# Attention and two gated layers on one core: loads of queries, keys and values moved to POOL's queue, and the order at the last stage's start and end changed

## The chip, the cores and the metric

The kernel runs on one core of a Trainium2 chip. The metric is the device time of one execution in microseconds (us). The median of three runs is 1690.28 us.

## What is computed

All arrays are float32. There are 8 x 576 = 4608 tokens with 8 heads of 64 columns; attention looks only inside chunks of 64 tokens. Its output goes through a layer with a squared relu and then through a layer with a gate.

```
scores = scale * np.matmul(q_c, k_c.transpose(0, 1, 2, 4, 3))      # chunks of 64 x 64
attn = np.exp(scores - max); attn = attn / (sum + 1e-09)
x = attn @ v_c                                   # 4608 x 512
h = np.maximum(x @ w_in, 0.0);  x = h * h @ w_out        # w_in 512 x 2048, w_out 2048 x 512
g = x @ w_gate;  val = x @ w_val                 # 512 x 1536 each
out = (g * (1.0 / (1.0 + np.exp(-g))) * val) @ w_out2    # 1536 x 512
```

## The kernel before

The 4608 tokens are nine blocks of 512. `sets` holds block 0 alone and then four pairs of blocks; a pair is worked on together, since its product with a weight is made by a scheme of seven products for eight (roles 1 to 7 of a `Pair`, and in the last stage roles 1, 5, 6, 2, 7, 4, 3 in `Last`). Every float32 product is three matmuls of 128x512 (lines 464 to 466: high weight by high data, low by high, high by low), so each operand is first split into `hi` (ACT, line 154) and `lo` (DVE, line 157).

The stages follow each other: a start in which the weights w_in are prepared and block 0 and the first pair go through attention; the up product with w_in for each set, and *beside* it the attention of the set after it; the down product with w_out; the products with w_gate and w_val; and the last stage with w_out2 (`Last`). Results between stages go through memory: `g` by ACT's DMA queue, nearly everything else by SP's.

Attention works on units of 256 tokens, four to a pair of blocks. For a unit, `attn_qk` loads q and k (line 324, 512 KB each), `attn_products` makes the scores s by 64 small matmuls (line 340), DVE and ACT make e from it, POOL multiplies e by the reciprocal sums (line 372, e<-e,rec), DVE transposes e to z and ACT copies it to p, with four small DMAs p<-z (line 419), `attn_v` loads v (line 329), and `attn_values` makes the outputs xps by 64 small matmuls (line 439). The table `WHEN` and the function `attention_step` say beside which quarter of which weight each of these steps stands; `EARLY` is 6, the number of units in block 0 and the first pair, which are done in the start. Units from 6 on belong to the second, third and fourth pair: 12 units.

PE's order is that of the code (`ordered(ET.PE)`). On the other engines and on the DMA queues a scheduler sets the order when the program is built; each engine and each queue then runs its row strictly in that order, and an entry that waits holds up all behind it. SP's row holds, beside the loads of q, k and v, the loads W<-wi of prepared weights (line 230, `load_combo`, 1792 KB, asked for by `Products.ask`), which wait until PE has done with the buffer, the stores wi<-W of weights (line 223) and the p<-z copies.

The last stage takes its operands from memory (`Last.load`, line 875, tiles h) and its weights V by `load_last` (lines 285 and 291). `Last.make` builds the operands of the product that comes next; `take`, made by `turned_out`, adds (line 518, o), transposes to z (line 847), and stores the finished half in four DMAs (line 853).

Of the kernel before, what the change touches and what calls it, by code (L numbers as in the profile page):

```python
# [28 lines left out]
def attention_mlp_mlp_kernel(  # L29
# [29 lines left out]
    nc = tc.nc  # L59
# [11 lines left out]
    sets = [(0,)] + [(b, b + 1) for b in range(1, nb, 2)]  # L71
# [12 lines left out]
    def duo(name, dtype=F32):  # L84
        return big.tile([P, 2, BLOCK], dtype, tag="big", name=name)

    def one(name):
        return small.tile([P, BLOCK], F32, tag="t", name=name)
# [191 lines left out]
    def load_last(product, apart=False):  # L280

        r = ROLES[product]
        if not apart:
            v = wp.tile([P, n2, 2, half], F32R, tag="W", name="V")
            nc.sync.dma_start(out=v.bitcast(F32), in_=vdram[r])
            last_weights[product] = [v[:, i] for i in range(n2)]
            return
        last_weights[product] = []
        for i in range(0, n2, 2):
            v = big.tile([P, 2, 2, half], F32R, tag="big", name="V")  # L290
            nc.sync.dma_start(out=v.bitcast(F32), in_=vdram[r][:, i:i + 2])
            last_weights[product] += [v[:, 0], v[:, 1]]

    class Work:
# [5 lines left out]
        def add(self, steps):  # L300
            self.queue.append(steps)
# [15 lines left out]
    EARLY = upb * (1 + len(sets[1]))  # L317
    at, vs = {}, {}
    xraw = {}

    def attn_qk(u):
        tiles = [duo("q"), duo("k")]
        for t, src in zip(tiles, (q, k)):
            nc.sync.dma_start(out=t, in_=src[2 * u:2 * u + 2].rearrange("n p c -> p n c"))
        at[u] = tiles

    def attn_v(u):
        vt = duo("v")
        nc.sync.dma_start(out=vt, in_=v[2 * u:2 * u + 2].rearrange("n p c -> p n c"))
        vs[u] = vt  # L330

    def attn_products(u):
# [128 lines left out]
    def three(ps, left, right, first, last, on=False):  # L461

        (lh, ll), (rh, rl) = left, right
        nc.tensor.matmul(out=ps, lhsT=lh, rhs=rh, start=first, stop=False, skip_group_check=on)  # L464
        nc.tensor.matmul(out=ps, lhsT=ll, rhs=rh, start=False, stop=False, skip_group_check=on)  # L465
        nc.tensor.matmul(out=ps, lhsT=lh, rhs=rl, start=False, stop=last, skip_group_check=on)  # L466

    def block_product(ps, w, i, x, first, last, on=False):
        for c in range(2):
            cols = slice(c * P, (c + 1) * P)  # L470
            three(
                ps,
                (w[:, 0, ROLES[i], cols], w[:, 1, ROLES[i], cols]),
                (x[0][:, c, :], x[1][:, c, :]),
                first and c == 0,
                last and c == 1,
                on,
            )
# [41 lines left out]
    class Pair:  # L520
# [6 lines left out]
        def product(self, ps, i, first):  # L527
            block_product(ps, self.w, i, self.ops[i], first, True, not first)
# [201 lines left out]
    up1 = Products(keys1, moving1, 2, 1, lambda key: squared)  # L730

    def x_sums(n):
        up1.ops[n] = Operands()
        up1.ops[n].sums([xraw.pop(b) for b in sets[n]])
# [103 lines left out]
    def turned_out(bs):  # L838
        z = [[big.tile([P, BLOCK // SQ, 2, SQ], F32, tag="big", name="z") for _ in range(2)] for _ in bs]
        left = [[2, 2] for _ in bs]  # L840

        def take(i, j, e, ps, r):
            if r is not None:
                o = one("o")
                add(o, ps, r)
                ps = o
            nc.vector.transpose(out=z[j][e][:, :, i, :], in_=ps.rearrange("p (b t) -> p b t", t=SQ))
            left[j][e] -= 1
            if left[j][e] == 0:
                rows = out[bs[j] * BLOCK:(bs[j] + 1) * BLOCK, :]  # L850
                rows = rows.rearrange("(b r) (q e c) -> q e r b c", r=SQ, q=4, e=2)
                for qd in range(4):
                    nc.sync.dma_start(
                        out=rows[qd, e],
                        in_=z[j][e][qd * SQ:(qd + 1) * SQ].rearrange("p b i t -> p b (i t)"),
                    )

        return take
# [4 lines left out]
    class Last:  # L863
# [37 lines left out]
                }[p])  # L901
            self.ops[n, p] = ops

        def product(self, ps, n, p, op, first, last=True, on=False):
            w, ops = last_weights[p], self.ops[n, op]
            for i in range(n2):
                hi, lo = ops[i // 2]
                for e in range(2):
                    cols = slice(e * P, (e + 1) * P)
                    three(  # L910
                        ps[e],
                        (w[i][:, 0, cols], w[i][:, 1, cols]),
                        (hi[:, i % 2, :], lo[:, i % 2, :]),
                        first and i == 0,
                        last and i == n2 - 1,
                        on,
                    )
# [14 lines left out]
        def run(self, m):  # L932
            n, p = self.seq[m]
            if p == 1:
                self.take = turned_out(sets[n])
            if len(sets[n]) == 1:
                if p == 1:
                    self.y = self.two("py")
                    self.product(self.y, n, 1, 1, True, False)
                elif p == 5:  # L940
                    self.y1 = self.two("py")
                    self.product(self.y1, n, 5, 1, True, False)
                elif p == 2:
                    self.product(self.y, n, 2, 2, False)
                    self.take_all(0, 0, self.y, None)
                else:
                    self.product(self.y1, n, 4, 4, False)
                    self.take_all(1, 0, self.y1, None)
            elif p == 1:
                self.x = self.two("px")  # L950
                self.product(self.x, n, 1, 1, True)
                self.r1 = self.kept(self.x, "r1")
            elif p == 5:
                self.z = self.two("pz")
                self.product(self.z, n, 5, 5, True)
            elif p == 6:
                self.product(self.x, n, 6, 6, False, on=True)
                self.u2 = self.kept(self.x, "u2")
            elif p == 2:
                y = self.two("py")  # L960
                self.product(y, n, 2, 2, True)
                self.take_all(0, 0, y, self.r1)
            elif p == 7:
                self.product(self.x, n, 7, 7, False, on=True)
                self.take_all(1, 1, self.z, self.kept(self.x, "u3"))
            elif p == 4:
                self.product(self.x, n, 4, 4, False, on=True)
                self.take_all(1, 0, self.x, None)
            else:
                self.product(self.z, n, 3, 3, False, on=True)  # L970
                self.take_all(0, 1, self.z, self.u2)

    down1, down2 = Down(g1dram, n1), Last()

# [24 lines left out]
    def beside1(n, m):  # L999
        def at_quarter(i):  # L1000
            t = 4 * m + i
            attention_step(n + 1, t)
            attention_step(n + 2, t - LAST)
            if t == 2:
                up1.ops[n].make(3)
            if n + 1 < len(sets):
                if t == 24:
                    x_sums(n + 1)
                if t - LAST in OPS:
                    up1.ops[n + 1].make(*OPS[t - LAST])  # L1010
            else:
                if t % 2 == 0:
                    work.step(1)
                if t == LAST - 8:
                    down1.begin()
                if t == LAST - 4:
                    down1.split(0)

        return at_quarter
# [104 lines left out]
    last = down2  # L1124
    load_last(2)
    load_last(4)
    load_last(6)
    with ordered(ET.PE):
        for m, (n, p) in enumerate(last.seq):
            if n + 1 < len(sets):  # L1130
                after = sets[n + 1]
                if p == 1:
                    last.load(after[0], 0)
                elif p == (4 if n else 2):
                    last.load(after[1], 0)
                elif p == 3 or (n == 0 and p == 4):
                    last.load(after[1], 1)
                    last.load(after[0], 1)
            if m == 1:
                load_last(7, True)  # L1140
                load_last(3, True)
            if m + 1 < len(last.seq):
                last.make(*last.seq[m + 1])
            last.run(m)
# [50 lines left out]
```

## Time and profile before

| | |
|---|---|
| median of three runs | 1690.28 us (1689.44 to 1691.79) |
| profiled execution, its own time | 1691.04 us |
| its span, first to last instruction | 1689.3 us |
| PE busy | 1610.9 us, 95% |
| DVE busy | 1018.0 us, 60% |
| ACT busy | 817.1 us, 48% |
| POOL busy | 130.7 us, 8% |
| mean granted clock of TensorE | 0.98 |

A busy PE is one with a matmul in flight; where PE stands, the trace names what ended the wait. The granted clock is either full or half; half means that a matmul of 128x512 starts every 0.43 us and not every 0.23. All times in the rows below are from the start of the span.

### The profile page before, as it was taken

How to read it: one execution, taken by the hardware profiler on the slowest of the kernel's cores; microseconds unless marked ns; L12 is line 12 of the kernel's file. 1: busy time of each engine (PE TensorE's matmuls, PEld its weight loads, DVE VectorE, ACT ScalarE, POOL GpSimd, SP SyncE). 2: the span in 40 equal slices, each digit the busy share in tenths (PEclk: the TensorE clock that was granted, in tenths of full speed). 3: DMA queues.
4: the chain of work that ended last, by engine and by line, in shares of the span. 5: the costliest groups of instructions: out<-in, count | busy, mean ns of one | idle time of the engine just before them, and what ended most of it. 6: DMA issues, size and time to landing. Idle time of an engine off the chain costs nothing.

```text
span 1689.3 us, 23605 instructions
## 1 busy us (share of the span) xinstructions
PE 1610.9 (95%) x9408; PEld 1326.7 (79%) x9408; DVE 1018.0 (60%) x1268; ACT 817.1 (48%) x1165; POOL 130.7 (8%) x94
## 2 busy tenths in 40 slices
PE   3868999989999999999999999999999999999997
PEld 3756777878888888888888888888888887788886
DVE  7883465554458657653222545546547996787884
ACT  5774676767876434433112433434335653334441
POOL 3220001010112111110000000000000110000000
PEclk8888999999999999999999999999999999999999
DMA  8555777696976867784417876676578999563342
GB/s 332 218 219 209 256 282 270 244 317 231 337 251 220 301 242 268 273 310 173 131 42 273 312 244 221 227 285 221 195 259 284 380 390 397 214 199 117 104 142 50
DMA packets 140367, 407.10 MB, mean 241 GB/s; under 512 B 47840, under 2 KB 57056, under 8 KB 128736
## 3 DMA queue, kind: packets, MB, share of 16 engines
q1 hardware_dynamic: 129888, 367.83, 61.5%
q10 hardware_dynamic: 10368, 37.75, 5.9%
q8 instruction: 74, 1.21, 0.3%
q14 instruction: 37, 0.30, 0.1%
HBM read 278.92 MB, written 123.47 MB: 238 GB/s over the span
## 4 chain that ended last, share of the span: by engine, by line
PE 85%; DMA 6%; DVE 5%; issue 1%; ACT 1%; SPq 1%; POOL 0%; DVEq 0%; ACTq 0%; POOLq 0%
PE px L464 10%; PE px L466 10%; PE px L465 10%; PE acc L465 6%; PE acc L464 6%; PE acc L466 6%; PE py L464 5%; PE pz L464 5%; PE pz L466 5%; PE pz L465 5%; PE py L466 5%; PE py L465 5%; DMA k<-in_k_dram 4%; PE accs L465 2%; PE accs L464 2%; PE accs L466 2%
## 5 line engine op out<-in xcount | busy, mean ns | idle before, releaser
L464 PE MATMUL px<-hi,W 128*128 128x512 f32 x640 | 252.1, 394 | 7.4 <-ACT hi L154 5.5
L466 PE MATMUL px<-lo,W 128*128 128x512 f32 x640 | 250.4, 391 | 3.6 <-DVE lo L157 3.6
L465 PE MATMUL px<-hi,W 128*128 128x512 f32 x640 | 250.1, 391 | 0.0
L139 POOL TENSOR_TENSOR m<-m,raw 128x512 int32<-128x512 int32 x68 | 93.8, 1396 | 989.8 <-ACT r L532 557.8
L532 ACT COPY u<-px 128x512 f32<-128x512 f32 x160 | 92.4, 578 | 148.0 <-PE px L466 147.5
L464 PE MATMUL acc<-hi,w 128*128 128x512 f32 x416 | 161.8, 389 | 0.0
L465 PE MATMUL acc<-hi,w 128*128 128x512 f32 x416 | 161.8, 389 | 0.0
L466 PE MATMUL acc<-lo,w 128*128 128x512 f32 x416 | 161.5, 389 | 0.0
L464 PEld LDWEIGHTS px<-hi,W 128*128 128x128 f32 x640 | 120.7, 189 | 35.4 <-ACT hi L154 6.3
L466 PEld LDWEIGHTS px<-lo,W 128*128 128x128 f32 x640 | 120.8, 189 | 29.6 <-DVE lo L157 4.4
L518 DVE TENSOR_TENSOR g<-pz,u 128x512 f32<-128x512 f32 x112 | 76.9, 687 | 109.9 <-PE pz L466 73.1
L157 DVE TENSOR_TENSOR lo<-graw,hi 128x1024 fp32r<-128x1024 f32 x72 | 91.4, 1270 | 82.1 <-PE acc L465 42.8
L465 PEld LDWEIGHTS px<-hi,W 128*128 128x128 f32 x640 | 120.7, 189 | 24.7
L154 ACT CAST hi<-h 128x1024 fp32r<-128x1024 f32 x93 | 95.3, 1053 | 90.6 <-DVE h L885 21.4
L633 DVE TENSOR_TENSOR g<-g,sig 128x1024 f32<-128x1024 f32 x54 | 66.0, 1221 | 119.3 <-ACT sig L632 119.2
L464 PE MATMUL py<-hi,W 128*128 128x512 f32 x320 | 128.8, 403 | 0.4 <-DMA W<-wv 0.4
L464 PE MATMUL pz<-hi,W 128*128 128x512 f32 x320 | 125.7, 393 | 1.3 <-DVE g L518 1.2
L465 PE MATMUL py<-hi,W 128*128 128x512 f32 x320 | 126.4, 395 | 0.0
L466 PE MATMUL py<-lo,W 128*128 128x512 f32 x320 | 126.4, 395 | 0.0
L465 PE MATMUL pz<-hi,W 128*128 128x512 f32 x320 | 125.2, 391 | 0.0
L466 PE MATMUL pz<-lo,W 128*128 128x512 f32 x320 | 125.0, 391 | 0.0
L157 DVE TENSOR_TENSOR lo<-h,hi 128x1024 fp32r<-128x1024 f32 x93 | 110.2, 1215 | 10.3 <-ACT hi L154 7.9
(123 smaller groups left out, 3116.1 us busy)
## 6 DMA issues: line engine op xcount, KB each, us to landing
W<-wv SPq DMA_DIRECT2D x30, 1792.0 KB, 8.6
g<-g ACTq DMA_DIRECT2D x72, 512.0 KB, 4.9
graw<-g SPq DMA_DIRECT2D x72, 512.0 KB, 4.3
W<-wi SPq DMA_DIRECT2D x20, 1792.0 KB, 9.4
W<-wg SPq DMA_DIRECT2D x20, 1792.0 KB, 8.3
h<-g SPq DMA_DIRECT2D x54, 512.0 KB, 8.1
h<-h SPq DMA_DIRECT2D x54, 512.0 KB, 6.3
raw<-in_w_out_dram SPq DMA_DIRECT2D x28, 512.0 KB, 8.1
```

The lines of the kernel that those rows point to most:

```text
L139: nc.gpsimd.tensor_tensor(out=mi[:, t, :], in0=mi[:, t, :], in1=word(raw, 0, I32), op=ALU.add)
L154: nc.scalar.copy(out=hi, in_=src)
L157: nc.vector.tensor_tensor(out=lo, in0=src, in1=hi, op=ALU.subtract)
L464: nc.tensor.matmul(out=ps, lhsT=lh, rhs=rh, start=first, stop=False, skip_group_check=on)
L465: nc.tensor.matmul(out=ps, lhsT=ll, rhs=rh, start=False, stop=False, skip_group_check=on)
L466: nc.tensor.matmul(out=ps, lhsT=lh, rhs=rl, start=False, stop=last, skip_group_check=on)
L518: nc.vector.tensor_tensor(out=o, in0=ps, in1=r, op=ALU.add)
L532: nc.scalar.copy(out=r, in_=self.x)
L633: nc.vector.tensor_tensor(out=g[j], in0=g[j], in1=s, op=ALU.mult)
```

## The change

The loads of q, k and v of units from 6 on are issued by POOL and not by SP. In the up stage, the explicit early split of operand 3 (`make(3)`) is gone; the split is then made where product 3 first asks for it. In the last stage, the weights of product 6 are loaded one step later, those of 7 and 3 two steps later, and the data of the first pair one step earlier. The last product of the last set is made for one half of its columns first (all of e = 0, then all of e = 1), each half taken as soon as it is there, and for the last set every other output DMA is issued by ACT.

```
+    def loader(u):
+        return nc.sync if u < EARLY else nc.gpsimd
+
     def attn_qk(u):
         tiles = [duo("q"), duo("k")]
         for t, src in zip(tiles, (q, k)):
-            nc.sync.dma_start(out=t, in_=src[2 * u:2 * u + 2].rearrange("n p c -> p n c"))
+            loader(u).dma_start(out=t, in_=src[2 * u:2 * u + 2].rearrange("n p c -> p n c"))
...
-        nc.sync.dma_start(out=vt, in_=v[2 * u:2 * u + 2].rearrange("n p c -> p n c"))
+        loader(u).dma_start(out=vt, in_=v[2 * u:2 * u + 2].rearrange("n p c -> p n c"))
...
-                    nc.sync.dma_start(
+                    (nc.scalar if qd % 2 and bs == sets[-1] else nc.sync).dma_start(
...
-            else:
+            elif n + 1 < len(sets):
                 self.product(self.z, n, 3, 3, False, on=True)
                 self.take_all(0, 1, self.z, self.u2)
+            else:
+                for e in range(2):
+                    self.product(self.z, n, 3, 3, False, on=True, es=(e,))
+                    self.take(0, 1, e, self.z[e], self.u2[e])
...
-            if t == 2:
-                up1.ops[n].make(3)
...
-    load_last(6)
...
-                elif p == (4 if n else 2):
+                elif p == (4 if n else 5):
                     last.load(after[1], 0)
-                elif p == 3 or (n == 0 and p == 4):
+                elif p == (3 if n else 2):
                     last.load(after[1], 1)
                     last.load(after[0], 1)
             if m == 1:
+                load_last(6)
+            if m == 3:
                 load_last(7, True)
                 load_last(3, True)
```

SP's row before, from the first store of a weight in the second pair's attention on (wi and W are prepared weights, q, k and v the loads in question, p<-z the small copies):

```order
L223 DMA wi_1402<-W 128x3584
L324 DMA k<-in_k_dram 128x2x512
L324 DMA q<-in_q_dram 128x2x512
L324 DMA k<-in_k_dram 128x2x512
L329 DMA v<-in_v_dram 128x2x512
L419 DMA p<-z 32x512 x3
L230 DMA W<-wi_694 128x3584
L419 DMA p<-z 32x512
L324 DMA q<-in_q_dram 128x2x512
L324 DMA k<-in_k_dram 128x2x512
L329 DMA v<-in_v_dram 128x2x512
L230 DMA W<-wi_1103 128x3584
```

In that place of SP's row only the weights and the p<-z copies are left, and the loads stand in POOL's row, between its multiplications of e. POOL's row now, for the same pair (its lines are those of the changed kernel: 327 and 332 are 324 and 329 of before, 375 is 372):

```order
L327 DMA q<-in_q_dram 128x2x512
L327 DMA k<-in_k_dram 128x2x512
L327 DMA q<-in_q_dram 128x2x512
L327 DMA k<-in_k_dram 128x2x512
L375 TENSOR_TENSOR e<-e,rec 128x1024
L332 DMA v<-in_v_dram 128x2x512
L327 DMA q<-in_q_dram 128x2x512
L327 DMA k<-in_k_dram 128x2x512
L332 DMA v<-in_v_dram 128x2x512
L375 TENSOR_TENSOR e<-e,rec 128x1024
L327 DMA q<-in_q_dram 128x2x512
L327 DMA k<-in_k_dram 128x2x512
```

Before, POOL's row had nothing but the multiplications there; now q and k of a pair's first two units stand ahead of the first multiplication, four loads (v, q, k, v) stand between the first and the second, three between the second and the third, and one before the fourth. The third and fourth pair have the same pattern.

ACT's row at the start of the last stage, before (hi is the high half of an operand, r the kept copy of the first product of the first pair):

```order
L632 ACTIVATE sig<-g_11447 128x1024
L154 CAST hi<-h 128x1024 x9
L922 COPY r_11927<-px 128x512
L154 CAST hi<-h 128x1024
L922 COPY r_11928<-px 128x512
L154 CAST hi<-h 128x1024 x9
```

And now:

```order
L635 ACTIVATE sig<-g_11447 128x1024
L154 CAST hi<-h 128x1024 x12
L925 COPY r_11927<-px 128x512
L925 COPY r_11928<-px 128x512
L154 CAST hi<-h 128x1024 x7
```

The three casts for the product that follows stand ahead of the two copies of r, and no longer between and behind them.

## Rows read from the trace of the kernel before

**Rows 1.** The page: PE's clock in 40 slices, and the chain that ended last by engine.
```profile
PEclk8888999999999999999999999999999999999999
...
PE 85%; DMA 6%; DVE 5%; issue 1%; ACT 1%; SPq 1%; POOL 0%; DVEq 0%; ACTq 0%; POOLq 0%
```
**Rows 2.** PE's waits from 120 to 400: total us, times, longest.
```profile
PE s L340 <- DMA k<-in_k_dram: 17.2, 6, 6.0
...
PE px L464 <- DMA W<-wi: 1.3, 1, 1.3
```
**Rows 3.** SP's queue before the first of them: start, us, what it issues.
```profile
122.31 0.32 SPq L223 DMA_DIRECT2D wi<-W  x1
122.72 0.39 SPq L324 DMA_DIRECT2D k<-in_k_dram  x1
```
**Rows 4.** SP's queue before the third, and its longest wait over the span.
```profile
236.25 0.34 SPq L230 DMA_DIRECT2D W<-wi  x1
...
237.14 0.68 SPq L324 DMA_DIRECT2D k<-in_k_dram  x1
...
SPq L230 <- PE pz L466: 287.9, 47, 11.1
```
**Rows 5.** Stretches: PE, PEld, DVE, ACT, POOL busy us, clock, DMA share, GB/s.
```profile
131.70:137.40 5.70, 5.70 (x73) 4.81 (x74) 3.64 (x4) 1.06 (x1) 0.00 (x0) 0.50 0.74 275
...
179.60:181.50 1.90, 0.01 (x1) 0.04 (x1) 0.69 (x1) 1.44 (x3) 0.00 (x0) 1.00 0.99 307
181.80:185.20 3.40, 3.40 (x64) 2.90 (x57) 1.83 (x2) 1.51 (x2) 0.00 (x0) 0.50 1.03 360
...
274.40:276.20 1.80, 0.04 (x4) 0.07 (x5) 0.69 (x1) 1.39 (x3) 0.00 (x0) 1.00 0.95 329
...
367.10:369.40 2.30, 0.00 (x0) 0.00 (x0) 0.68 (x1) 1.89 (x3) 0.00 (x0) 1.00 0.90 300
369.60:372.90 3.30, 3.30 (x68) 2.89 (x66) 1.43 (x2) 1.19 (x2) 0.00 (x0) 0.50 1.07 377
```
**Rows 6.** The chain of waits in order of time: a matmul of 128x512 at either clock.
```profile
137.68 0.23 PE px L464
...
144.59 0.43 PE px L464
```
**Rows 7.** POOL's last weight work, then the scores of two units and e between.
```profile
107.01 3.43 POOL L139 TENSOR_TENSOR m<-m,raw 128x512 int32<-128x512 int32 x2 [8.86 <-ACT W L154]
...
236.15 1.16 PE L340 MATMUL s<-k,q 64*64 64x64 f32 x64
...
244.73 1.91 POOL L372 TENSOR_TENSOR e<-e,rec 128x1024 f32<-128x1024 f32 x1 [53.46 <-DVE rec L371]
...
249.76 1.79 PE L340 MATMUL s<-k,q 64*64 64x64 f32 x64 [2.70 <-DMA k<-in_k_dram]
```
**Rows 8.** The eight loads k from 200 to 400: us from issue to landing.
```profile
DMA to landing us min/median/max: 5.4/11.0/12.5
```
**Rows 9.** Start of the last stage: ACT, then PE's waits from 1440 to 1470.
```profile
1454.23 0.59 ACT L922 COPY r<-px 128x512 f32<-128x512 f32 x1 [12.09 <-PE px L466]
1454.71 1.05 ACT L154 CAST hi<-h 128x1024 fp32r<-128x1024 f32 x1
...
PE pz L466 <- DVE lo L157: 1.6, 2, 1.1
PE pz L464 <- ACT hi L154: 0.9, 1, 0.9
```
**Rows 10.** The end: DVE, SP's queue, and the page's time to landing.
```profile
1679.84 1.37 DVE L518 TENSOR_TENSOR o<-pz,u 128x512 f32<-128x512 f32 x2 [6.76 <-PE pz L466]
1681.12 1.29 DVE L847 STREAM_TRANSPOSE z<-o 128x512 f32<-128x512 f32 x2
1681.85 4.62 SPq L853 DMA_DIRECT2D out_dram<-z  x8
...
out_dram<-z SPq DMA_DIRECT2D x72, 128.0 KB, 2.7
```

More of the change, by code (lines that the diff above doesn't have):

```diff
@@ L902, in make, with product @@
             self.ops[n, p] = ops
-        def product(self, ps, n, p, op, first, last=True, on=False):
+        def product(self, ps, n, p, op, first, last=True, on=False, es=range(2)):
             w, ops = last_weights[p], self.ops[n, op]
@@ L907, in product @@
                 hi, lo = ops[i // 2]
-                for e in range(2):
+                for e in es:
                     cols = slice(e * P, (e + 1) * P)
```

## The prediction

> **What bounds the kernel now.** I read the page's chain first: 85% of what ended last is PE, so the 15% that is not are stretches in which PE stands, and only those can be won without taking matmuls away; the clock line says that PE's clock is down early in the span [rows 1]. PE's waits come next. The whole stretch beside which the second to fourth pair go through attention, 120 to 400, has one large entry: six waits of the scores for a load of k, 17.2 us, the longest 6.0 [rows 2]. These loads are what the change moves. Then SP's queue ahead of such a wait. At 122.31 SP issues the store of a weight, and 0.41 us later the k that PE lacks [rows 3]: k was not late because its buffer was taken, it stood behind a store that waited for DVE's last weight. At 236.25 the load W of a weight goes out, and k 0.9 us behind it [rows 4]; W is the entry of SP's queue with the largest wait, 287.9 us for PE to free its buffer, so what stands behind a W goes when W goes, and then moves its 512 KB behind W's 1792 KB. Last, the stretches around the stalls: behind each but one of the six the clock is at half, 1.2 instead of 2.4 GHz, for 3.3 to 5.7 us [rows 5].
>
> **The change, part by part.** *Stalls removed.* All six waits are for k of units that now load through POOL: the first unit of the second pair, the fourth of the same, and the second and fourth of each later pair. POOL's row has no store and no W in it. For a pair's first two units q and k stand ahead of the first multiplication: POOL ends its last weight work at 110.4, and PE wants the first of these k at 125.7 [rows 5, 7], 15 us later; a load of k took 5.4 to 12.5 us [rows 8]. The wait goes: 17.2 us.
>
> *Clock given back.* The half-speed stretches behind the stalls last 5.7, 3.4 and three times 3.3 us, five in all, of which the first two and the last are shown [rows 5]; sum 19.0. A matmul takes 0.43 us there and 0.23 at full speed [rows 6], so 19.0 x (0.43 - 0.23) / 0.43 = 8.8 us are lost. PE did not stand ahead of them for any other reason, so they go with the stalls.
>
> *POOL pays for the loads.* 36 loads are added to a row that is nearly empty. The trace has no load issued by POOL. Below, it costs 0.4 us, what SP needs for the same issue [rows 3]; above, 1.9 us, a pass of POOL over as large a tile [rows 7]. I take the middle, 1.2: POOL writes addresses of rows, not numbers, but by program. From one unit's scores to the next PE takes 249.76 - 236.15 - 2.70 = 10.9 us [rows 7]; in that time POOL has at most one multiplication, 1.9, and four loads, 4.8: 6.7 us, hidden in 10.9. It stays hidden up to (10.9 - 1.9) / 4 = 2.25 us a load. The tightest is the third unit of a pair: its k stands behind the first multiplication and behind v and q. That multiplication begins 8.6 us after its unit's scores (244.73 - 236.15), the third scores come 21.8 after them; 21.8 - 8.6 - 1.9 leaves 11.3 us for three loads, 3.6, and the landing. I take 7 us for that, nearer the 5.4 than the 11.0 of rows 8, since no W is ahead of it in its own queue: 10.6 of 11.3, no stall, and 0.7 us to spare. The k of the fourth unit, behind the second multiplication and q, has 8.9 us.
>
> The Trainium skill, page "DMA: Bandwidth & Descriptors", section "Issuing engines are not separate DMA queues", says that DMAs started by different engines run on the same 16 DMA engines and interleave, so that a second issuer saves only issuing time. The trace shows those engines full in the stalls, a share of 0.90 to 0.99 [rows 5], which agrees; by that rule moving a load wins only where it is issued earlier.
>
> *W comes later.* What q, k and v no longer leave to W, W shares. PE waited for W once, 1.3 us [rows 2]. Between nothing and three such waits more, 0 to 4; I take 1.0.
>
> *Cover lost.* During the stalls of the fourth units ACT was busy 1.44, 1.39 and 1.89 us [rows 5], 4.7 in all, on outputs of earlier products, and PE needs the banks that ACT empties. Without the stall PE meets this work. Between 0 and 4.7; I take 3.5, since ACT was busy for three quarters of these stalls.
>
> *Early split of operand 3 removed.* One cast on ACT and one subtraction on DVE per pair move behind others. They are asked for beside the next weight, one unit's scores to the next, about 10 us later; PE's matmuls cover it, cost nothing. Without that cover it is a cast of 1.05 us [rows 9] and a subtraction of about the same per pair.
>
> *Start of the last stage.* ACT's cast of the second product's operand stood behind the copy of r, which waits for the end of the first product [rows 9]. PE then waits 0.9 for the cast and 1.6 for the halves that follow. Now three casts stand ahead of the copies. 2.5 us go. The weights that are loaded later are wanted by the third product of the pair or later, more than 10 us on.
>
> *The end.* Before, the second half of the last product is added by 1681.21, and SP, from 1681.85 on, issues eight stores in 4.62 us, to 1686.47 [rows 10]. Now the first half is stored while PE makes the second. The second half's sum again ends at 1681.2, its transpose takes half of 1.29, to 1681.86, and four stores follow, two on each of two queues at 4.62 / 8 = 0.58: to 1683.0. The landing behind it stays 2.7. That is 3.4 us less; I take 3.3.
>
> *Sum.* -17.2 - 8.8 + 1.0 + 3.5 - 2.5 - 3.3 = -27.3 us. Against the profiled execution, 1691.0, that is 1663.7; the median of the runs is 0.7 us below that execution, so 1663.0.
>
> **The rivals.** *The third unit's k becomes late.* If a load costs 2.4 us on POOL, three cost 7.2, with 7 us of landing 14.2 of the 11.3: 2.9 us of stall in each of three pairs and about 1.5 us of half clock behind each: 13 us given back, 1676; with half of that 1670. For it: the 0.7 us to spare. Against it: 5.4 us is the fastest landing. Such a price would come about if POOL's issuing stood still while DVE works: from 131.7 on DVE is busy 3.64 of 5.70 us [rows 5], so 1.2 us could become 1.2 x 5.70 / 2.06 = 3.3, and 2.4 lies between. The Trainium skill, page "SBUF — State Buffer", section "Who interferes with whom", says that a DMA issued by GpSimd is held up while VectorE runs a copy or a scalar operation in a two-port mode; no run here shows it so far, and beside attention DVE has nearly only operations that the section leaves out.
>
> *The change doesn't reach the data.* If the new buffers come free no earlier than SP's turn came, the same bytes move in the same full stretches, the six stalls stay, and only the start of the last stage and the end are won: 1690.3 - 5.8 = 1684.5. Against it: k went 0.41 us behind the store [rows 3], with no wait of its own left.
>
> *POOL becomes the bound: slower.* A POOL row is strict: a multiplication that stands behind four loads is late by what they cost. Above 2.25 us a load the second multiplication slips by four times the excess, above (10.9 - 1.9) / 3 = 3.0 the third by three times. What is won, 27, is used up at 9 us a pair: 4 x (g - 2.25) + 3 x (g - 3.0) = 9 gives g = 3.9 us. At 5 us it is 11 + 6 = 17 a pair, 51 in all: 1663 + 51 = 1714. For it: nothing in the trace bounds the program that makes the addresses. Against it: 3.9 us is twice POOL's work on every number of such a tile.
>
> **How the numbers follow.** The forecast (1656 to 1671) gets 0.62, the late third k (1671 to 1680) 0.17, the data not reached (near 1684.5) 0.08, no change that can be told 0.04, POOL as the bound 0.09. A measurement of this kernel tells some 0.2%, 3.4 us, from no change. Faster is the sum of the first three, 0.87; the same 0.04; slower 0.09. The range runs from 1656, where the two added costs, 4.5, and some 2 us more of clock are not paid, to 1680, the end of the late third k, and holds 0.79.
>
> **What would show it.** PE's waits for k between 120 and 400 gone or below 2 us in all, and no half clock behind scores; POOL's row shows the loads at 1 to 2 us each, its multiplications not later after their scores than 8.6 us; PE's first wait behind a fourth unit's scores is for ACT; none at the start of the last stage; last output landed some 4.5 us behind PE's end and not 8. I am wrong if PE waits for k or for xps with a DMA or POOL as the releaser in every pair, or if W takes the place of k in PE's waits.

## The result and the profile after

The changed kernel takes 1663.72 us, median of 4 runs (1659.39 to 1666.39), beside 1691.03 for the kernel before on the same chip: a ratio of 0.9836, 95% interval 0.9812 to 0.9859. It is faster by 27.3 us. The profiled execution took 1663.95 us, its span 1662.2. Of the executions behind the ratios below, one (of the kernel before without the early split) took 3281.5 us for a reason that no record shows, and its ratio leaves it out.

The page after, the two rows that answer to [rows 1]:

```profile
PEclk8889999999999999999999999999999999999999
...
PE 89%; DVE 5%; DMA 3%; ACT 1%; issue 1%; POOL 0%; SPq 0%; ACTq 0%; POOLq 0%; DVEq 0%
```

PE holds 89% of the chain and not 85%. PE's waits from 120 to 400, which answer to [rows 2] (total us, times, longest):

```profile
PE px L469 <- DVE lo L157: 3.2, 2, 2.6
PE px L467 <- DMA W<-wi: 1.7, 1, 1.7
PE px L467 <- ACT hi L154: 1.6, 1, 1.6
```

The six waits for k, 17.2 us, are gone; the wait for W grew from 1.3 to 1.7. The waits for `hi` and `lo` end between 121.8 and 138.0 and were there before (1.6 and 3.6 us). POOL's row in the third pair (start, us, what it does, and in brackets how long it stood and for what); the first line is the k of the second unit, one of the six that were late:

```profile
221.07 0.72 POOL L327 DMA_DIRECT2D k<-in_k_dram  x1
...
233.86 1.89 POOL L375 TENSOR_TENSOR e<-e,rec 128x1024 f32<-128x1024 f32 x1 [12.07 <-DVE rec L374]
235.71 0.74 POOL L332 DMA_DIRECT2D v<-in_v_dram  x1
236.45 0.72 POOL L327 DMA_DIRECT2D q<-in_q_dram  x1
237.17 0.72 POOL L327 DMA_DIRECT2D k<-in_k_dram  x1
237.89 0.72 POOL L332 DMA_DIRECT2D v<-in_v_dram  x1
245.21 1.90 POOL L375 TENSOR_TENSOR e<-e,rec 128x1024 f32<-128x1024 f32 x1 [6.60 <-DVE rec L374]
247.06 0.74 POOL L327 DMA_DIRECT2D q<-in_q_dram  x1
247.80 0.72 POOL L327 DMA_DIRECT2D k<-in_k_dram  x1
```

A load costs POOL 0.72 to 0.75 us (one of the 36 took 0.87), and after four of them POOL still stands 6.6 us until DVE's `rec`: the multiplication is not held up by the loads. All six k that were late are issued earlier now: before, 3.0 to 9.9 us ahead of the moment at which PE wanted them, and now 13.2 to 17.0 us. From issue to landing they took 8.8, 8.9, 12.5, 10.1, 12.2 and 10.6 us before and take 8.5, 6.0, 6.5, 10.3, 6.4 and 10.9 now. With the old landing times each would still be in time, so the earlier issue is enough by itself. The k in the first line, which went out 0.9 us behind a W before [rows 4], took 12.5 us then and takes 6.5 now (minimum, median and maximum of this one load):

```profile
DMA to landing us min/median/max: 12.5/12.5/12.5
...
DMA to landing us min/median/max: 6.5/6.5/6.5
```

Taken together the eight k between 200 and 400 land little faster, to be set beside [rows 8], since others meet a W instead: the four that go out on POOL's queue within 1.2 us of a W on SP's, ahead of it or behind it, take 10.3 to 12.0 us, the other four 6.4 to 9.4.

```profile
DMA to landing us min/median/max: 6.4/9.8/12.0
```

The start of the last stage, ACT, which answers to [rows 9]: the casts stand ahead of the copy of r, and PE waits for nothing from 1420 to 1450.

```profile
1427.92 1.06 ACT L154 CAST hi<-h 128x1024 fp32r<-128x1024 f32 x1 [1.67 <-PE px L468]
1430.64 1.06 ACT L154 CAST hi<-h 128x1024 fp32r<-128x1024 f32 x1 [1.66 <-DVE h L888]
1432.87 1.27 ACT L925 COPY r<-px 128x512 f32<-128x512 f32 x2 [1.17 <-PE px L469]
```

The end, DVE, then ACT's queue, then SP's, which answer to [rows 10]: the second half of the last product is added by 1655.86 and turned by 1656.61, and its four stores are issued by 1657.57, two on each queue.

```profile
1655.17 0.69 DVE L521 TENSOR_TENSOR o<-pz,u 128x512 f32<-128x512 f32 x1 [2.64 <-PE pz L469]
1655.90 0.71 DVE L850 STREAM_TRANSPOSE z<-o 128x512 f32<-128x512 f32 x1
...
1649.17 8.40 ACTq L856 DMA_DIRECT2D out_dram<-z  x5
...
1656.64 0.85 SPq L856 DMA_DIRECT2D out_dram<-z  x2
```

PE's order is the same in both kernels but for the last product of the last set, so each matmul can be set beside its counterpart. After minus before: +2.6 us ahead of the second pair's first scores, -22.7 behind the fourth pair's attention, -21.4 ahead of the last stage, -25.4 behind its start, -27.1 at the end.

### The profile page after: what moved, and what is told of

It is laid out like the page before. It is cut to its first block, busy times and chain, and to the rows that moved or that the text cites. A ratio compares the mean times of both kernels' runs of the same rounds, so it can differ in the third digit from the quotient of the medians.

```text
span 1662.2 us, 23648 instructions
## 1 busy us (share of the span) xinstructions
PE 1602.5 (96%) x9408; PEld 1320.0 (79%) x9408; DVE 1021.9 (61%) x1268; ACT 816.4 (49%) x1165; POOL 156.5 (9%) x130
## 4 chain that ended last, share of the span: by engine, by line
PE 89%; DVE 5%; DMA 3%; ACT 1%; issue 1%; POOL 0%; SPq 0%; ACTq 0%; POOLq 0%; DVEq 0%
PE px L467 11%; PE px L469 11%; PE px L468 11%; PE acc L469 6%; PE acc L468 6%; PE acc L467 6%; PE pz L469 5%; PE pz L467 5%; PE pz L468 5%; PE py L467 5%; PE py L468 5%; PE py L469 5%; PE accs L469 2%; PE accs L468 2%; PE accs L467 2%; DMA raw<-in_w_out_dram 1%
## 5 line engine op out<-in xcount | busy, mean ns | idle before, releaser
L467 PE MATMUL py<-hi,W 128*128 128x512 f32 x320 | 126.6, 396 | 0.3 <-DMA W<-wv 0.3
L468 PE MATMUL py<-hi,W 128*128 128x512 f32 x320 | 124.7, 390 | 0.0
```

## The experiments

Ratios are to the kernel before, on the same chip, with 95% intervals.

**The loader alone, and everything but the loader.** The first is the kernel before with only this edit, the second the changed kernel without it:

```
-            nc.sync.dma_start(out=t, in_=src[2 * u:2 * u + 2].rearrange("n p c -> p n c"))
+            (nc.sync if u < EARLY else nc.gpsimd).dma_start(out=t, in_=src[2 * u:2 * u + 2].rearrange("n p c -> p n c"))
```

> The kernel before with one edit: q, k and v of units from 6 on go through POOL's queue. My theory: all of the gain between 120 and 400 us comes from this edit, because k no longer stands in SP's row behind stores and loads W that wait. It expects PE's six waits for k gone, PE between the first scores of the second pair and 400 us some 25 us ahead of before, the four waits of some 2.9 us in all at the start of the last stage unchanged, the end unchanged, and about 1690.5 - 25 + (0 to 3 at the start) = 1665 to 1669 us. Rival: part of it comes from the early split of operand 3 that the change removed (ACT and DVE freed for the scores); then waits for ACT or DVE of 1 us or more per pair stand beside attention and the time is above 1672.

1674.71 us, ratio 0.9891 (0.9866 to 0.9916). Its profiled execution took 1667.95, inside what was expected; the median is not. It is above the rival's 1672, but the rival's waits for ACT or DVE in every pair are not there. The waits from 120 to 400:

```profile
PE px L466 <- DVE lo L157: 4.1, 2, 3.0
PE px L464 <- DMA W<-wi: 3.4, 1, 3.4
PE px L464 <- ACT hi L154: 1.6, 1, 1.6
PE xps L439 <- DMA p<-z: 1.4, 2, 1.0
```

The loader by itself takes away every wait for k. It also leaves more behind than the whole change does: 3.4 us for W, and 1.4 for p.

> The changed kernel with the loads back on SP: only the edits in the up stage (no early split of operand 3), at the start of the last stage and at the end are left. My theory: the six waits for k stay at 17 us in all with the half clock behind them, and only the start of the last stage (4 us by the traces so far) and the end (1.7 us) are won: 1691.0 - 5.7 = 1685.3 us, within 2. Rival (removal of the early split matters for the loads, since SP's row is ordered anew): the waits for k change by more than 3 us either way.

1678.25 us, ratio 0.9912 (0.9886 to 0.9939), 7 us less than expected. The profiled execution took 1682.53 and has the six waits:

```profile
PE s L343 <- DMA k<-in_k_dram: 15.9, 6, 5.9
```

So the other edits are worth more than the 5.8 us that were counted for them. What they are worth apart is taken up below.

**Another queue, and an earlier place in SP's row.** Is it POOL's queue that helps, or the place in a row? First, the loads on ACT's queue:

```
-        return nc.sync if u < EARLY else nc.gpsimd
+        return nc.sync if u < EARLY else nc.scalar
```

> The changed kernel with the same 36 loads issued by ACT and not by POOL. If what counts is only that k does not stand in SP's row behind a store or a W, ACT's row does as well as POOL's, about 1664 us. My theory adds that the row which takes the loads must be one that can wait: ACT has some 75 of 100 us busy there and does casts and copies that PE waits for, and a load that waits there for its buffer, or a cast ahead of it that waits, holds up the rest. It expects new waits of PE for ACT or for k, 3 to 15 us in all between 120 and 400, so 1667 to 1679 us. A third outcome, near 1690, would say that POOL's own way of starting transfers is what helped.

1678.24 us, ratio 0.992 (0.9901 to 0.9938).

```profile
PE s L343 <- DMA k<-in_k_dram: 10.5, 6, 6.5
...
PE pz L469 <- DVE lo L157: 2.0, 2, 1.0
...
PE px L467 <- ACT r L535: 1.1, 2, 0.8
```

A queue without W is not enough: ACT's row has work and waits of its own ahead of the loads (the k of the third pair's second unit goes out 8.3 us before PE wants it, and from POOL 17.0), k is late behind it in six places, and PE waits for ACT's copies and for DVE's `lo` besides. Then all loads on SP, but asked for earlier:

```
-        return nc.sync if u < EARLY else nc.gpsimd
+        return nc.sync
...
-    WHEN = {"qk": (-3, 2, 6, 10), "scores": (2, 6, 10, 14), "turn": (6, 10, 14, 18), "out": (11, 15, 19, 23)}
+    WHEN = {"qk": (-4, 1, 5, 9), "scores": (2, 6, 10, 14), "turn": (6, 10, 14, 18), "out": (11, 15, 19, 23)}
```

> The changed kernel with the loads back on SP, but q and k are asked for one quarter of a weight earlier. In SP's row the fourth unit's k of each pair then stands ahead of a W and no longer behind it, and so does the second unit's of the third and fourth pair; the first unit's k of the second pair still stands behind the waiting store. If place in the row is the cause (my theory), the five later waits go (11.2 us) with their half clock, and the first, 6.0 us, stays: 1685.3 - 11.2 - 5.9 = some 1668 us, 1666 to 1672. Rival: k needs a queue of its own, because on SP's queue its bytes move behind W's 1792 KB whatever is issued first; then waits for k of 8 us or more in all stay behind the first, and the time is above 1674.

1666.51 us, ratio 0.9851 (0.9836 to 0.9866).

```profile
PE s L343 <- DMA k<-in_k_dram: 5.3, 1, 5.3
...
PE px L467 <- DMA W<-wi: 1.1, 1, 1.1
```

Exactly the five waits that were named are gone and the one behind the store is left, without POOL. The place in the row, and with it the time of issue, is the cause; a queue of its own is not needed, and the rival falls: on SP's queue the k of the third and fourth pair's fourth units lands in 5.4 and 5.8 us, since no W goes out within 5 us of it.

**The early split of operand 3, and the ends.** Four kernels: the kernel before without the early split; the changed kernel with loads on SP and the split kept, so that only the ends of the last stage are changed; the changed kernel with the split put back; and the same with all stores of the last set on SP as well. The lines in question:

```
             if t == 2:
                 up1.ops[n].make(3)
...
-                    (nc.scalar if qd % 2 and bs == sets[-1] else nc.sync).dma_start(
+                    nc.sync.dma_start(
```

> The kernel before with the early split of operand 3 taken out and nothing else. The prediction counted this at nothing: within 2 us of before, six waits for k of some 17 us in all, no new wait of 1 us. Rival, from the runs with all edits but the loader, which took 1674 to 1683 us where 1685 was expected: the early split costs 4 us or more where it stands, and the time is 1688 us or less, with shorter waits for k or with the operand's halves ready earlier.

1684.58 us, ratio 0.9955 (0.9939 to 0.9971).

```profile
PE s L340 <- DMA k<-in_k_dram: 14.6, 6, 5.9
```

Not nothing: 7.6 us by the ratio. In the profiled execution, which at 1689.09 us lies above the median, the waits for k are 2.6 us shorter.

> The changed kernel with the loads on SP and the early split of operand 3 put back: only the edits at the start and the end of the last stage are left. By the traces so far these are worth 4.0 and 1.7 us: before - 5.7, 1684 to 1686 us, six waits for k of 15 to 18 us in all. The runs with all edits but the loader took 1678 us; if the excess of 7 us is due to the early split on SP's row, as the kernel before without it (1684.6) says, it is missing here. Rival: the excess came from the ends; then 1677 to 1680 us here as well.

1680.29 us, ratio 0.9944 (0.9923 to 0.9964): 9.5 us by the ratio, more than the 5.7 expected, with 6.1 at the interval's near end. Its profile shows the ends as expected: no wait at the start of the last stage, and 2.2 us less behind PE's last matmul. The expectation that the excess would be missing here was at best half right: the time is that of the rival's upper end.

> The changed kernel with only the early split of operand 3 put back. If the early split costs time only through the waits for k on SP's queue, it costs little where k is on POOL's: 1664 to 1666 us, with no wait for k. Rival: it costs its 7 us here too, by ACT's or DVE's work: 1670 to 1672 us.

1666.91 us, ratio 0.9865 (0.9842 to 0.9888), between the two theories' bounds and nearer the first. No wait for k; but these two, where the changed kernel has 1.7 and none:

```profile
PE px L467 <- DMA W<-wi: 3.7, 1, 3.7
...
PE xps L442 <- DMA p<-z: 1.6, 2, 0.8
```

> The changed kernel with two edits put back, far apart in time: the early split of operand 3, and all stores of the last set on SP (the last product stays split into halves). End: the prediction gave the second queue half of the stores' time, 1.2 us. The trace of the changed kernel shows its last four stores on two queues landing 4.26 us behind the first issue, and the last four on one queue before the change took 4.38 us: so the second queue is expected to be worth 0.1 us and not 1.2, because the stores share the same engines. Early split: nothing by the prediction, 1664 us within 3; by the rival 4 to 7 us, 1668 to 1671, with waits for ACT or DVE beside attention.

1665.34 us, ratio 0.9846 (0.9826 to 0.9866). The end with all stores on SP, DVE and SP's queue:

```profile
1655.87 0.69 DVE L521 TENSOR_TENSOR o<-pz,u 128x512 f32<-128x512 f32 x1 [2.64 <-PE pz L469]
1656.59 0.71 DVE L850 STREAM_TRANSPOSE z<-o 128x512 f32<-128x512 f32 x1
...
1651.68 7.62 SPq L856 DMA_DIRECT2D out_dram<-z  x9
```

And the last four stores there, with their median from issue to landing:

```profile
out_dram<-z SPq DMA_DIRECT2D x4, 128.0 KB, 2.5
```

From the start of the second half's sum to the end of the span (1662.6) it is 6.7 us, and with two queues in the changed kernel 1662.2 - 1655.17 = 7.0. There the last four took 3.1 us to landing on SP's queue and 3.3 on ACT's:

```profile
out_dram<-z SPq DMA_DIRECT2D x2, 128.0 KB, 3.1
out_dram<-z ACTq DMA_DIRECT2D x2, 128.0 KB, 3.3
```

The second queue gives nothing; what the end won came from the split into halves. In the nine profiles with two queues the last store lands 4.0 to 4.3 us behind the transpose, and on one queue 4.0. The Trainium skill, page "DMA: Bandwidth & Descriptors", section "Issuing engines are not separate DMA queues", says that DMAs interleave on the same 16 engines whichever engine starts them, and that several issuers save only the time to start them. The trace agrees: issuing the four took 1.0 us behind the transpose and not 2.0 (1657.30 to 1659.30), and in the median they landed 0.6 to 0.8 us later after their issue.

**A dearer POOL.** POOL fills each tile of the 36 loads with zeros ahead of its load, once in the first kernel and three times in the second. For q and k, and for v alike:

```
+            if u >= EARLY:
+                for _ in range(1):
+                    nc.gpsimd.memset(t, 0.0)
             loader(u).dma_start(out=t, in_=src[2 * u:2 * u + 2].rearrange("n p c -> p n c"))
```

> The changed kernel, in which POOL first fills the tile of each of the 36 loads with zeros, so that a load costs POOL 0.72 us and a fill, by the nearest row (1.9 us for a multiplication of such a tile) 1 to 2 us: 1.7 to 2.7 us in all. By the prediction it stays hidden up to 2.25 us, and above 2.4 the third unit's k of each pair becomes late, some 13 us in all. So 1664 us within 3 if the measured price is below 2.25, and 1670 to 1680 if it is 2.4 to 2.8, with the waits at the third units. If waits come at other units, the sum that the prediction made of POOL's row was wrong.

1675.0 us, ratio 0.9909 (0.989 to 0.9928). The price is 0.72 + 0.97, 1.7 us a load, below 2.25, and still 11 us are lost. POOL, then SP's queue:

```profile
251.63 0.97 POOL L329 MEMSET k<- 128x1024 f32 x1
252.53 0.72 POOL L330 DMA_DIRECT2D q<-in_q_dram  x1
253.24 0.72 POOL L330 DMA_DIRECT2D k<-in_k_dram  x1
...
251.92 0.33 SPq L230 DMA_DIRECT2D W<-wi  x1
```

PE's waits from 120 to 400:

```profile
PE s L349 <- DMA k<-in_k_dram: 5.2, 2, 2.8
PE px L473 <- DMA W<-wi: 4.3, 1, 4.3
```

That k's time from issue to landing:

```profile
k<-in_k_dram POOLq DMA_DIRECT2D x1, 512.0 KB, 13.0
```

The waits are at the fourth units of the third and fourth pair, not at the third units, whose k is 0.2 and 0.3 us ahead of the scores. At the fourth unit of the third pair W goes out on SP's queue at 251.92, 1.3 us ahead of k on POOL's, and k then takes 13.0 us to land. In the changed kernel k goes out at 247.80, ahead of the W at 248.96, and lands in 10.3. There k went out 13.2 us ahead of its use and had 3.0 to spare; here it goes out 10.8 us before PE wants it and lands 2.7 us slower, and only the two together make it late. That a W which has just gone out stretches k's landing across queues the changed kernel shows as well (11.2 and 12.0 us for two k issued 1.1 us behind a W), so POOL's price counts also by what it lets k meet. The scheduler has moved one v behind the second multiplication in this kernel, so it is not the price alone that differs, and the third unit's k has one load fewer ahead of it.

> The same with three fills ahead of each load: 3.7 to 6.4 us a load for POOL. The prediction's third rival says that POOL becomes the bound and that the gain is used up at 3.9 us a load; at 5 us 1714 us. So slower than before if the price is above 4, with waits for k at second to fourth units and for POOL's multiplication; if the time stays below 1680, POOL's row has far more slack than the sum gave it.

1699.76 us, ratio 1.0051 (1.0031 to 1.007), at 0.72 + 3 x 0.9 = 3.4 us a load: slower than before, at a price below the 3.9 that the prediction gave for it. Here the scheduler has put several loads behind multiplications.

```profile
PE s L349 <- DMA k<-in_k_dram: 19.5, 7, 3.5
PE px L473 <- DMA W<-wi: 5.3, 1, 5.3
```

POOL in the third pair, with the k that PE then lacks for 3.5 us, the second unit's:

```profile
243.14 1.90 POOL L381 TENSOR_TENSOR e<-e,rec 128x1024 f32<-128x1024 f32 x1 [10.21 <-ACT r L541]
...
245.89 0.74 POOL L330 DMA_DIRECT2D k<-in_k_dram  x1
```

POOL stood 10.2 us ahead of the multiplication, with this k behind it in the row; it is not POOL's work that makes this k late but its place in POOL's row. All seven late k are issued some 5 us before their scores and land in 4.7 to 5.6. Ahead of this pair's next two multiplications POOL stood only 3.4 and 3.9 us, so there its work has a part. The kernel mixes the price with the cause that SP's row had before; at which price alone POOL becomes the bound is not shown.

**Both together.** q and k a quarter earlier on SP, as above, and only the second pair's first two units on POOL:

```
-        return nc.sync if u < EARLY else nc.gpsimd
+        return nc.gpsimd if u in (EARLY, EARLY + 1) else nc.sync
...
+    WHEN = {"qk": (-4, 1, 5, 9), "scores": (2, 6, 10, 14), "turn": (6, 10, 14, 18), "out": (11, 15, 19, 23)}
```

> The changed kernel with q, k and v of only the first two units of the second pair on POOL's queue, all others back on SP, and q and k asked for one quarter of a weight earlier, as in the run with SP alone. By my theory the only wait for k left there, 5.3 us for the first unit behind the waiting store, goes too, with the half clock behind it (some 1.5 to 3 us): 1666.5 - 5.3 - 2 = 1659 us, 1656 to 1662, a few us below the changed kernel. Rival: the earlier q and k take their share of SP's queue from W, so that a wait for W of 3 us or more takes the place: then 1662 to 1666, no better than the changed kernel.

1660.72 us (1659.21 to 1661.60), ratio 0.9819 (0.9798 to 0.9839). It is the lowest median of all, 3 us below the changed kernel, though the intervals of the two overlap. No wait for k, and W's is 1.2:

```profile
PE px L469 <- DVE lo L157: 3.1, 2, 2.6
PE px L467 <- ACT hi L154: 1.6, 1, 1.6
PE px L467 <- DMA W<-wi: 1.2, 1, 1.2
```

## Why the prediction was right, and where its terms were off

Forecast were 1663.0 us and -27.3; measured 1663.72 and -27.3. The mechanism was right. Several terms were not, and that they made up for each other is luck.

*Stalls removed, -17.2.* Right, and shown to be due to the place in the row: the earlier issue alone would have been enough for all six, and on SP alone with an earlier place five of the six waits go. Three of the six k also land 2.9 to 6.0 us sooner, away from W; the prediction had said that k moves behind W's bytes, but gave this no part in the gain.

*Clock given back, -8.8.* The half-speed stretches behind these stalls are gone in the changed kernel. But they do not always come: the kernel with everything but the loader has 15.9 us of the same waits, and its records show half clock behind three of the six (6.8, 3.4 and 3.4 us), which is 6.3 us by the same sum; the kernel with only the ends changed shows the same. Nor is it the same in each execution of one kernel: with everything but the loader the mean granted clock is 0.983 in the profiled execution and 0.986 to 0.988 in the other three, which took 1 to 8 us less.

*POOL's price, 1.2 a load.* Measured 0.72, nearest the lower bound, SP's 0.4. Nothing was held up. The third unit's k was feared to have 0.7 us to spare; it landed 9.4 us after its issue at 237.17, not 7, and was there 2.3 us ahead of the scores at 248.86: three loads were 1.4 us cheaper than taken, and the multiplication came 7.2 us behind its unit's scores and not 8.6. The fourth unit's k is as tight, with 3.0 and 2.3 us to spare in the two later pairs: it goes out 13.2 us ahead of its scores, where 8.9 had been left for its landing, but it lands in 10.3 and 10.9, because the sum left out that a W on the other queue stretches the landing. In the kernel with one fill this k was the late one. The bound of 2.25 us a load, which the expectation for that kernel used, did not fit the prediction's own tightest place either: with 11.3 us for three loads and 7 of landing the third unit's k is late above 1.4.

*W comes later, +1.0.* Here +0.4; in the three kernels with the loads on POOL and the early split kept, the wait is 3.0 to 3.7 in place of 1.3. But PE goes on at 153.2, 153.2 and 154.5 there and at 154.5 in the changed kernel, which reached this place 2 us later by its start (below): a part of that delay was hidden in this wait.

*Cover lost, +3.5.* Not paid: PE has no wait for ACT behind a fourth unit's scores, which was named as a sign.

*Early split, 0.* This step failed: its removal is a gain. Four comparisons give 7.6 us (the kernel before without it), 5 (everything but the loader beside the ends alone), 5 and 1.7 (the changed kernel beside those with the split put back, with ACT's stores and with SP's), each uncertain by 3 to 6. What of it a profile shows is 2.6 us of waits for k on SP, and 1.4 to 2.1 us of waits for p on POOL, which no kernel without the split has. By the mean granted clocks on record (0.9846 over seven executions without it, 0.9823 over 13 of the kernel before on the same chip) some 3.6 us of the 7.6 would be clock; this is an estimate, at 0.43 and 0.23 us a matmul. The way from the split to these waits, and to the clock, is not settled; in SP's row a W goes out in one place behind two p<-z copies where it went behind three, and no run took that apart.

*Start of the last stage, -2.5.* It gave 4.1. A wait that the trace gives as 0.94 us cost PE 1.33 - 0.23 from one matmul's start to the next, and 0.11 more at the matmul behind it: some 0.27 us around each of four waits, the fourth of which (0.39, for `lo`) was not counted.

*The end, -3.3.* It gave 1.7. The issuing went as worked out, 0.96 us behind the transpose; the landing did not stay, as the prediction put it, since the stores of two queues share what one had. From the last issue to the end of the span it is 4.6 us and was 2.8, and 1.5 of these 1.8 lie ahead of the last landing. The last output landed 5.8 us behind PE's end, before 7.8, and not some 4.5.

*Not foreseen.* The start was 2.6 us later, and one wait of 1.1 us stands at 1303.76 for ACT, where ACT waited for weights that landed 12 us after their issue; both are in code that the change does not touch.

Between the two profiles alone, PE gains 25.3 us over the loads' stretch, beside an execution of the kernel before that has half clock behind five of the six waits. Taken over all kernels the loader is worth 13 to 18 us by the medians and ratios (alone; beside everything else; beside the ends), each uncertain by some 5, not the 21.5 that its terms sum to; the ends 6 by the places in the traces, as forecast, and 4 to 10 by the ratios; the split some 5 and not 0. The forecast of the sum owes its closeness to this. The rivals: the change did reach the data, POOL did not become the bound at its real price, and the third unit's k was in time.

## What to carry to other kernels

A load that PE needs soon should not stand in a row behind an entry that waits; a queue helps only if its engine's row does not wait itself, and asking a quarter earlier on the old queue did nearly as much as the new one. Before a queue is added for speed, see whether its transfers meet a large one that is going or about to go: issued 1.3 us behind 1792 KB, 512 KB took 13.0 us on a queue of their own. A sum can be right by terms that cancel, so run the parts alone.

## What the runs showed of the hardware that was not expected

The stretches at half clock differ between executions of the same instructions. Behind the wait of 4.9 us that ends near 90, in code that all these kernels share, the clock is at half for some 3.4 us in the records of six kernels, the one before among them, and for some 6.8 in those of the other kernels with a profile. The rows for the stretch 93.2 to 96.5 are, before and after (us, PE, PEld, DVE, ACT and POOL busy, clock, DMA share, GB/s):

```profile
93.20:96.50 3.30, 3.30 (x89) 2.89 (x84) 2.47 (x4) 3.25 (x6) 1.72 (x1) 1.00 0.00 0
```

```profile
93.20:96.50 3.30, 3.30 (x89) 3.18 (x86) 2.87 (x5) 3.28 (x6) 1.33 (x1) 0.50 0.02 5
```

PE is busy throughout in both. At 0.43 and 0.23 us a matmul [rows 6] such a stretch is worth 1.6 us; the changed kernel had two more of them ahead of 127, one here and one behind the waits at 114 and 119, and was 2.6 us late there. Some of the 2 to 10 us by which executions of one kernel differ here seem to be of this kind: with everything but the loader those at 1674.4 and 1675.1 us have a mean granted clock of 0.987 and 0.988 and the one at 1682.5 has 0.983, at most 6 to 8 us at the same two rates, an estimate. It is not all: the fourth took 1681.4 at 0.986. So a difference of 3 us between two kernels is read from places in the traces, or from many runs, and not from one profile against another.
